# Loading and splitting the first part of two weight matrices in another place

## The chip, the cores and the metric

The kernel runs on one core of one Trainium2 chip, as a single program. The metric is the device time of one execution in microseconds (us). Before the change it is 689.38 us, the median of 3 runs (688.5 to 691.06).

## The reference

Two blocks work one after the other on an array of 2048 rows by 512 columns, both steered by a vector c (adaLN: shift, scale and gate come from `silu(c) @ w_mod`):

```
h = layernorm(u) * (1 + ca) + sa
x = u + ga * S4(h)                      # S4: per column a causal convolution of length 2048, K from A, B, C, dt; by FFT
h = layernorm(x) * (1 + cb) + sb
a  = gelu(layernorm(h) @ w1)            # 512 x 512
hs = shift(a) @ w2                      # four column groups, shifted by +1, -1, +2, -2 rows; 512 x 512
x1 = h + hs
y  = x1 + gelu(layernorm(x1) @ w3) @ w4 # 512 x 1376 and 1376 x 512
out = x + gb * y
```

All is float32. The matrix products with w1 to w4 are done in two parts: each float32 operand is split into a high part, rounded to the type that TensorE takes (fp32r), and a low part, the remainder, also fp32r; high times high, low times high and high times low are added up.

## The kernel before, in words

The order of all work is written out by hand: the program runs under manual scheduling, so each engine executes its instructions, and issues its DMAs, in the order of the source. A wait at the head of an engine's queue holds back all that is behind it on that engine.

In the first stage the kernel K of the convolution is made and u is normalized and transformed. In the second stage (`steps`, L1096 to L1153) 16 product steps run, 2 column halves by 8 blocks of frequencies: `spectrum_k` (L664) transforms K for a block from the tile VK[jh], with T2 and the flipped T3 as the other operand; `multiply` (L685) forms the complex product with the spectrum of u (tile us, two buffers); `back` (L695) transforms back over one axis and stores z to the DRAM array ZT, on POOL's queue, the last one in two parts on SP's and ACT's. `load_inv` (L717) brings the blocks of ZT (512 KB each, or halves of them) back as tiles ld, and `inv_half` (L726) does the inverse transform along the other axis, whose result VectorE adds to X2, the residual array. VK[1] and T3 lie in the pool c2, which lives until all inverse transforms are done; us, zc, z lie in the pool s2, which ends with the last product step (`s2x.close()`, L1154). SBUF is given to pools in stack order from two sides; pools with `reuse_waits="tile"` wait tile by tile for the last use of what lay there.

Behind L1154 the inverse transforms of the second half wait for the stores of the last step and the loads behind them. `inv_half(1, 3, 1)` reads blocks 0, 3, 4 and 7 of ZT, one half of each, and these four halves are the first that are loaded, two on SP's queue and two on ACT's (L1167 to L1169). `keep(n)` issues n matmuls whose result is not used. Then come the normalizations and `mix_half` (L929), the product with w1 for a group of 256 rows and half of the columns, its gelu into the tile go (pool gop, two buffers) and the store of go to the DRAM array GD on SP's queue.

From L1225 on w3 and w4 come in. Both stand in DRAM copies (WD). `weights` (L743) makes one pair of tiles for the high and the low part of a whole matrix; its `load` issues a DMA into the low tile and returns `split`, which copies the rounded value to the high tile on ACT (L755) and subtracts it in place on VectorE (L756). The loads, `load_w3(0)` to `load_w4(2)`, 23 in all, are issued on SP at L1230 to L1244, among the stores of go and the loads of `chan_load` (L870, the shifted rows from GD). The splits wait in a list, from which `split_w(n)` takes the next n: eight between L1255 and L1278, the other fifteen in the first channel group. `chan(g, r)` (L979), eight times, does the channel part for 256 rows: `chan_first` (w3, gelu), `chan_second` (w4).

The lines that the prediction's steps speak of:

```
        for k, i in ((3, 1), (0, 0)):
            load_inv(1, k, i, Y)
            load_inv(1, k + 4, i, S)
```

Of the kernel before, what the change touches and what calls it, by code (L numbers as in the profile page):

```python
# [7 lines left out]
F32 = mybir.dt.float32  # L8
# [98 lines left out]
def body(ctx, tc, A):  # L107
    nc = tc.nc
    V, S, P, T, Y = nc.vector, nc.scalar, nc.gpsimd, nc.tensor, nc.sync
# [10 lines left out]
    WD = {k: dpool.tile(list(A[k].shape), F32, name="D" + k) for k in ("w2", "w3", "w4")}  # L120
# [150 lines left out]
    f2 = lambda t: t.rearrange("p a b -> p (a b)")  # L271
# [234 lines left out]
    side = {k: [] for k in range(40)}  # L506
    for k in range(8):
        w, i = ("w3", k) if k < 4 else ("w4", k - 4)
        n = A[w].shape[0] // 4
# [37 lines left out]
    with tc.manual_schedule():  # L547
# [13 lines left out]
        for k in range(33):  # L561
# [8 lines left out]
            if k < 32:  # L570
# [3 lines left out]
                e = products(k)  # L574
# [22 lines left out]
        for f in later:  # L597
# [7 lines left out]
    c2 = a2.enter_context(pool("c2"))  # L605
# [1 line left out]
    Gm = c2.tile([128, 2, 64], F32, name="Gm")  # L607
    FI = c2.tile([128, 32, 2, 32], F32, name="FI")
    VK = [v0x.enter_context(pool("v0", side="right")).tile([128, 64, 2, 64], F32, name="VK0"),
          c2.tile([128, 64, 2, 64], F32, name="VK1")]  # L610
    ldp = a2.enter_context(pool("ldp", bufs=7))
    s2x = ExitStack()
    s2 = s2x.enter_context(pool("s2", bufs=2))
    psa = s2x.enter_context(pool("psa", bufs=2, space=PSUM))
    psb = s2x.enter_context(pool("psb", bufs=4, space=PSUM))
    kbank = lambda shape: psb.tile(shape, F32, name="pk2")
# [39 lines left out]
    t3s = {}  # L656

    def flip(kc):
        t = t3s[kc] = c2.tile([128, 8, 64], F32, name="T3", bufs=3)
        for gh in range(2):  # L660
            r = slice(gh * 64, gh * 64 + 64)
            P.tensor_scalar(t[r], T2[kc // 4][r, kc % 4 * 4:kc % 4 * 4 + 8, 64 - gh * 64:128 - gh * 64], -1.0, None, op0=OP.mult)
# [80 lines left out]
    def weights(pl, src, rows, cols, name, ntile):  # L743
        hi = pl.tile([128, ntile, cols], F32R, name=name + "h")
        lo = pl.tile([128, ntile, cols], F32R, name=name + "l")

        def load(stage, i, m=1, c0=0, c1=cols):
            n = min(128, rows - i * 128)
            w = stage(m, c1 - c0) if stage else lo.bitcast(F32)[:, i:i + m, c0:c1]
            Y.dma_start(w[:n], src[i * 128:i * 128 + (m - 1) * 128 + n, c0:c1].rearrange("(a p) n -> p a n", p=n))  # L750

            def split():
                for j in range(m):
                    h = hi[:n, i + j, c0:c1]
                    act(h, w[:n, j])  # L755
                    V.tensor_sub(lo[:n, i + j, c0:c1], w[:n, j], h.bitcast(F32))  # L756
            return split
        return hi, lo, load
# [24 lines left out]
    def half_stat(b, jh):  # L783
        V.bn_stats(st1[:, (b + 2) % 16, jh], X2[:, b, jh * 256:jh * 256 + 256])
# [50 lines left out]
    def three(p, wh, wl, hl, c):  # L835
        hi, lo = hl
        for k in range(4):
            T.matmul(p, wh[:, k, c], hi[k], start=(k == 0), stop=False)  # L838
            T.matmul(p, wl[:, k, c], hi[k], start=False, stop=False)  # L839
        for k in range(4):  # L840
            T.matmul(p, wh[:, k, c], lo[k], start=False, stop=(k == 3))  # L841
# [93 lines left out]
    def chan_first(hl, f2):  # L935
        p = psw.tile([128, 2, 256], F32, name="pm")
        ne, m = (2, 128) if f2 < 5 else (1, 96)
        for e in range(ne):
            c = slice((f2 * 2 + e) * 128, (f2 * 2 + e) * 128 + m)
            three(p[:m, e], W3h, W3l, hl, c)  # L940
        gf = c2p.tile([128, 2, 256], F32, name="gf")
        gh = c2p.tile([128, 2, 256], F32R, name="gh")
        gl = c2p.tile([128, 2, 256], F32R, name="gl")
        act(gh[:m, :ne], p[:m, :ne], AF.Gelu_apprx_tanh)
        act(gf[:m, :ne], p[:m, :ne], AF.Gelu_apprx_tanh)
        V.tensor_sub(gl[:m, :ne], gf[:m, :ne], gh[:m, :ne].bitcast(F32))  # L946
        return gh, gl, ne, m

    def second_high(acc, part, f2, i):
        gh, gl, ne, m = part  # L950
        s = slice(i * 128, i * 128 + 128)
        for e in range(ne):
            f = f2 * 2 + e
            T.matmul(acc[i], gh[:m, e, s], W4h[:m, f], start=(f == 0), stop=False)  # L954
            T.matmul(acc[i], gh[:m, e, s], W4l[:m, f], start=False, stop=False)  # L955

    def second_low(acc, part, f2, i):
        gh, gl, ne, m = part
        s = slice(i * 128, i * 128 + 128)
        for e in range(ne):  # L960
            f = f2 * 2 + e
            T.matmul(acc[i], gl[:m, e, s], W4h[:m, f], start=False, stop=(f == 10))  # L962

    def chan_second(acc, part, f2):
        for i in range(2):
# [113 lines left out]
            chan_out(g, acc, i, (Y,) if g < 7 else (Y, S))  # L1079
        return r  # L1080

    splits = []

    def load_w3(c):
        for i in range(4):
            splits.append(ldw3(None, i, 1, 512 * c, min(512 * c + 512, 1376)))

    def load_w4(c):
        for f in range(4 * c, min(4 * c + 4, 11)):
            splits.append(ldw4(None, f))  # L1090

    def split_w(n):
        for _ in range(n):
            splits.pop(0)()

    steps = [(jh, kc) for jh in range(2) for kc in range(8)]  # L1096
    with tc.manual_schedule():
# [11 lines left out]
        for n, st in enumerate(steps):  # L1109
            p = spectrum_k(*st)  # L1110
# [15 lines left out]
            if n % 2 == 0 and n < 14:  # L1126
                flip(steps[n + 2][1])
# [27 lines left out]
        tp = lambda name, bufs=1, **k: pool(name, bufs, reuse_waits="tile", **k)  # L1155
        cm = ctx.enter_context(tp("cm", 2, side="right"))
        hv = ctx.enter_context(tp("hv", side="right"))
        gop = ctx.enter_context(tp("gop", 2, side="right"))
        psT = ctx.enter_context(tp("psT", space=PSUM))
        psw = ctx.enter_context(tp("psw", 2, space=PSUM))  # L1160
        psy = a2.enter_context(tp("psy", 2, space=PSUM, side="right"))
# [12 lines left out]
            inv_half(0, 2, i, psy, "py")()  # L1174
        for b in (14, 15, 4, 5, 6, 7):
            half_stat(b, 0)
        for k in (1, 2):
            load_inv(1, k)
            load_inv(1, k + 4)
# [16 lines left out]
        hl = parts_of(transposed(mh.pop(7)[0]))  # L1196
# [10 lines left out]
        hl = parts_of(transposed(mh.pop(0)[0]))  # L1207
# [10 lines left out]
        hl = parts_of(transposed(mh.pop(1)[0]))  # L1218
# [4 lines left out]
        a2.close()  # L1223
        a12.close()
        pw34 = ctx.enter_context(tp("pw34"))  # L1225
        W3h, W3l, ldw3 = weights(pw34, WD["w3"], 512, 1376, "w3", 4)
        W4h, W4l, ldw4 = weights(pw34, WD["w4"], 1376, 512, "w4", 11)
        c2p = ctx.enter_context(tp("c2p", 2))
        psm = ctx.enter_context(tp("psm", 2, space=PSUM))
        load_w3(0)  # L1230
        mix_half(1, hl, 0)
        mix_norm(2)
        first_stats(3)
        mix_half(1, hl, 1)
        chan_load(0)
        load_w4(0)
        mix_mod1(3)
        mix_mod2(3, 0)
        hl = parts_of(transposed(mh.pop(2)[0]))
        mix_mod2(3, 1)  # L1240
        load_w3(1)
        load_w4(1)
        load_w3(2)
        load_w4(2)  # L1244
        mix_half(2, hl, 0)
        chan_split(0)
        mix_norm(3)
# [4 lines left out]
        add0()  # L1252
        hl = parts_of(transposed(mh.pop(3)[0]))
        add1 = chan_sum(0, 1)
        split_w(1)  # L1255
        n = cm.tile([128, 2, 512], F32, name="h2")
        sm = [(cm.tile([128, 2], F32, name="cmv"), cm.tile([128, 1], F32, name="crs")) for i in range(2)]

# [5 lines left out]
            V.tensor_scalar(n[:, i], cn[0][:, i], sm[i][0][:, 0:1], sm[i][1], op0=OP.subtract, op1=OP.mult)  # L1264

        stat0(0)
        split_w(1)
        add1()
        mix_half(3, hl, 0)
        stat0(1)  # L1270
        norm0(0)
        norm0(1)
        split_w(1)
        mix_half(3, hl, 1)
        r = transposed(n)
        split_w(1)
        r = parts_of(r)
        split_w(4)  # L1278
        chan_add(0)
        first_stats(4)  # L1280
        chan_load(1)
# [20 lines left out]
```

## Time and profile before

| | us |
|---|---|
| median of 3 runs | 689.38 |
| the profiled execution: its own time | 691.26 |
| the profiled execution: span | 689.5 |
| TensorE busy with matmuls | 642.6 (93%), 7195 instructions |
| VectorE (DVE) busy | 498.0 (72%), 795 |
| ScalarE (ACT) busy | 331.2 (48%), 505 |
| GpSimd (POOL) busy | 124.8 (18%), 236 |

A profile is one execution, recorded by the hardware. The span lies between the first and the last instruction recorded. PE is TensorE, PEld its weight loads, SP the queue that issues most DMAs. Busy time of a pipelined engine is not the same as use of its peak. The granted clock is the share of TensorE's full clock that it was given: 1.00 is 2.4 GHz, 0.50 is 1.2 GHz. The DMA share is the mean busy share of the core's 16 DMA engines. An arrow after a wait names what ended it as far as the profile can tell; of several things waited for it is the last by the profile, and where the one named can't have been waited for, it was another, often a DMA.

### The profile page before, as it was taken

How to read it: one execution, taken by the hardware profiler on the slowest of the kernel's cores; microseconds unless marked ns; L12 is line 12 of the kernel's file. 1: busy time of each engine (PE TensorE's matmuls, PEld its weight loads, DVE VectorE, ACT ScalarE, POOL GpSimd, SP SyncE). 2: the span in 40 equal slices, each digit the busy share in tenths (PEclk: the TensorE clock that was granted, in tenths of full speed). 3: DMA queues.
4: the chain of work that ended last, by engine and by line, in shares of the span. 5: the costliest groups of instructions: out<-in, count | busy, mean ns of one | idle time of the engine just before them, and what ended most of it. 6: DMA issues, size and time to landing. Idle time of an engine off the chain costs nothing.

```text
span 689.5 us, 16884 instructions
## 1 busy us (share of the span) xinstructions
PE 642.6 (93%) x7195; PEld 509.2 (74%) x7195; DVE 498.0 (72%) x795; ACT 331.2 (48%) x505; POOL 124.8 (18%) x236
## 2 busy tenths in 40 slices
PE   1899999999999998977998999999999999999996
PEld 0456655655569776634887889999899889898895
DVE  7899999999996887986987967464574536363522
ACT  3878988889875557432444623123131312222121
POOL 4011112112103355413741101001010000000000
PEclk9999999999999999998999999999999999999999
DMA  8603264643739997967387010020100201010001
GB/s 299 284 2 79 75 218 105 209 121 85 275 85 317 354 335 258 346 204 226 108 257 240 1 32 32 16 77 15 47 31 17 77 1 62 1 49 13 1 31 31
DMA packets 51091, 86.42 MB, mean 125 GB/s; under 512 B 4676, under 2 KB 39496, under 8 KB 48424
## 3 DMA queue, kind: packets, MB, share of 16 engines
q1 hardware_dynamic: 46712, 66.74, 30.1%
q0 software_dynamic: 3440, 17.57, 7.4%
q8 instruction: 56, 0.92, 0.6%
q10 hardware_dynamic: 864, 1.05, 0.5%
q14 instruction: 19, 0.16, 0.1%
HBM read 59.12 MB, written 32.90 MB: 133 GB/s over the span
## 4 chain that ended last, share of the span: by engine, by line
PE 70%; DVE 6%; DMA 5%; ACT 3%; POOL 2%; issue 1%; ACTq 0%; SPq 0%; DVEq 0%; POOLq 0%
PE pm L841 7%; PE pm L838 7%; PE pm L839 7%; PE xx L448 7%; PE pa L954 6%; PE pa L955 6%; PE pa L962 6%; PE kp L498 3%; DMA ZT<-z 3%; PE ph L893 2%; PE ph L895 2%; PE ph L892 2%; DMA ld<-ZT 2%; PE pu L426 2%; PE pT L803 2%; PE pk L626 2%
## 5 line engine op out<-in xcount | busy, mean ns | idle before, releaser
L115 ACT ACTIVATE gh<-pm 128x512 fp32r<-128x512 f32 (+1 forms) x48 | 26.9, 560 | 200.7 <-PE pm L841 200.7
L838 PE MATMUL pm<-nh,w3h 128*128 128x256 f32 (+1 forms) x352 | 86.6, 281 | 2.7 <-ACT nh L115 2.7
L839 PE MATMUL pm<-nh,w3l 128*128 128x256 f32 (+1 forms) x352 | 86.3, 280 | 0.1
L946 DVE TENSOR_TENSOR gl<-gf,gh 128x512 fp32r<-128x512 f32 (+1 forms) x48 | 30.8, 643 | 68.4 <-ACT gf L115 68.4
L954 PE MATMUL pa<-w4h,gh 128*128 128x512 f32 (+1 forms) x176 | 69.6, 395 | 0.0
L838 PEld LDWEIGHTS pm<-nh,w3h 128*128 128x128 f32 (+1 forms) x352 | 66.0, 187 | 4.4 <-ACT nh L115 2.9
L955 PE MATMUL pa<-w4l,gh 128*128 128x512 f32 (+1 forms) x176 | 68.9, 392 | 0.0
L839 PEld LDWEIGHTS pm<-nh,w3l 128*128 128x128 f32 (+1 forms) x352 | 65.9, 187 | 2.2 <-DVE w3l L756 0.5
L765 POOL TENSOR_TENSOR rs<-mv,eps_t 128x1 f32<-128x1 f32 (+1 forms) x39 | 11.0, 282 | 282.4 <-DVE mv L771 265.4
L841 PE MATMUL pm<-nl,w3h 128*128 128x256 f32 (+1 forms) x352 | 55.0, 278 | 0.0
L449 PE MATMUL xx<-MG,ON 64*128 64x512 f32 x160 | 48.1, 397 | 0.0
L962 PE MATMUL pa<-w4h,gl 128*128 128x512 f32 (+1 forms) x176 | 48.0, 390 | 0.0
L448 PE MATMUL xx<-MG,ON 64*128 64x512 f32 x160 | 48.0, 396 | 0.0
L841 PEld LDWEIGHTS pm<-nl,w3h 128*128 128x128 f32 (+1 forms) x352 | 47.0, 187 | 0.0
L898 DVE TENSOR_TENSOR h<-h,ph 128x512 f32<-128x512 f32 x16 | 11.0, 687 | 45.1 <-PE ph L895 45.1
L466 DVE SCALAR_TENSOR_TENSOR e<-tr,p 128x512 f32<-128x512 f32 x64 | 41.1, 684 | 1.5 <-ACT tr L115 1.5
L498 PEld LDWEIGHTS kp<-e,e 128*32 128x32 f32 x2048 | 30.1, 110 | 12.7 <-issue 7.6
L475 DVE TENSOR_TENSOR e<-tr,p 128x1024 f32<-128x1024 f32 x32 | 39.0, 1220 | 0.0
L476 DVE TENSOR_TENSOR e<-tr,m 128x1024 f32<-128x1024 f32 x32 | 39.0, 1219 | 0.0
L115 ACT ACTIVATE p<-xx 128x1024 f32<-128x1024 f32 (+1 forms) x40 | 37.5, 979 | 2.2 <-PE xx L252 1.0
L962 PEld LDWEIGHTS pa<-w4h,gl 128*128 128x128 f32 (+1 forms) x176 | 33.0, 188 | 7.3 <-DVE gl L946 0.2
L115 ACT ACTIVATE tr<-xx 128x1024 f32<-128x1024 f32 x32 | 33.0, 1030 | 9.6 <-PE xx L449 7.9
(236 smaller groups left out, 1731.6 us busy)
## 6 DMA issues: line engine op xcount, KB each, us to landing
VU<-vs SPq DMA_DIRECT2D x64, 128.0 KB, 3.7
ld<-VU SPq DMA_DIRECT2D x16, 512.0 KB, 7.4
ZT<-z POOLq DMA_DIRECT2D x30, 256.0 KB, 6.2
ld<-ZT SPq DMA_DIRECT2D x12, 512.0 KB
Dw<-in_w POOLq DMA_DIRECT2D x8, 688.0 KB, 4.7
xu<-in_u SPq DMA_DIRECT2D x4, 1024.0 KB, 8.0
KX<-in_x SPq DMA_DIRECT2D x4, 1024.0 KB, 8.0
GD<-go SPq DMA_DIRECT2D x16, 256.0 KB, 2.3
```

The source lines that it names most:

```text
L115: return S.activation(out, in_, f, bias=bias, scale=scale)
L448: T.matmul(x[:, :512], la, ma, start=(i == 0), stop=(i == len(ops) - 1))
L449: T.matmul(x[:, 512:], lb, mb, start=(i == 0), stop=(i == len(ops) - 1))
L466: V.scalar_tensor_tensor(e0[:, 1, a], tr[:, 1, 0], 1.0 - 2.0 * a, mg[:, a], op0=OP.mult, op1=OP.mult)
L475: V.tensor_mul(e0[:, 0], tr[:, 0, 0:1].to_broadcast([128, 2, 512]), mg)
L498: T.matmul(kp[32 * j:32 * j + 32, (k % 2) * 4 + g], e1[:, r, d], e0[:, r, :, d * 32:d * 32 + 32], start=(r == 0), stop=(r == 1), skip_grou ...
L838: T.matmul(p, wh[:, k, c], hi[k], start=(k == 0), stop=False)
L839: T.matmul(p, wl[:, k, c], hi[k], start=False, stop=False)
L841: T.matmul(p, wh[:, k, c], lo[k], start=False, stop=(k == 3))
L954: T.matmul(acc[i], gh[:m, e, s], W4h[:m, f], start=(f == 0), stop=False)
L955: T.matmul(acc[i], gh[:m, e, s], W4l[:m, f], start=False, stop=False)
L962: T.matmul(acc[i], gl[:m, e, s], W4h[:m, f], start=False, stop=(f == 10))
```

## The change

VK[1] and T3 move from c2 to s2, so that their place is free when the last product step ends. w3 and w4 are no longer one pair of tiles each but three, for 512, 512 and 352 columns (w3) or rows (w4). The first pair of each gets a pool of its own, pw3a, on the right side behind gop, opened right after the last product step. Its eight loads, 256 KB each, are issued there: w3's four on POOL's queue, w4's four on ACT's, ahead of the loads of the inverse transform. All eight are split by `split_w(8)` behind the half statistics that fill the time until those loads land. The other pairs are loaded on SP where they were, and the eight calls of `split_w` ahead of the channel groups are gone.

```diff
     VK = [v0x.enter_context(pool("v0", side="right")).tile([128, 64, 2, 64], F32, name="VK0"),
-          c2.tile([128, 64, 2, 64], F32, name="VK1")]
+          None]
...
+    VK[1] = s2.tile([128, 64, 2, 64], F32, name="VK1", bufs=1)
...
-        t = t3s[kc] = c2.tile([128, 8, 64], F32, name="T3", bufs=3)
+        t = t3s[kc] = s2.tile([128, 8, 64], F32, name="T3", bufs=3)
...
-        def load(stage, i, m=1, c0=0, c1=cols):
+        def load(stage, i, m=1, c0=0, c1=cols, q=Y):
...
-            Y.dma_start(w[:n], src[i * 128:i * 128 + (m - 1) * 128 + n, c0:c1].rearrange("(a p) n -> p a n", p=n))
+            q.dma_start(w[:n], src[i * 128:i * 128 + (m - 1) * 128 + n, c0:c1].rearrange("(a p) n -> p a n", p=n))
...
-            c = slice((f2 * 2 + e) * 128, (f2 * 2 + e) * 128 + m)
-            three(p[:m, e], W3h, W3l, hl, c)
+            f = f2 * 2 + e
+            three(p[:m, e], *W3[f // 4][:2], hl, slice(f % 4 * 128, f % 4 * 128 + m))
...
-    def load_w3(c):
+    splits, W3, W4 = [], [], []
+
+    def load_w3(pl, q=Y):
+        c0 = 512 * len(W3)
+        c1 = min(c0 + 512, 1376)
+        W3.append(weights(pl, WD["w3"][:, c0:c1], 512, c1 - c0, f"w3{c0}", 4))
         for i in range(4):
-            splits.append(ldw3(None, i, 1, 512 * c, min(512 * c + 512, 1376)))
-
-    def load_w4(c):
-        for f in range(4 * c, min(4 * c + 4, 11)):
-            splits.append(ldw4(None, f))
+            splits.append(W3[-1][2](None, i, q=q))
+
+    def load_w4(pl, q=Y):
+        r0 = 512 * len(W4)
+        r1 = min(r0 + 512, 1376)
+        W4.append(weights(pl, WD["w4"][r0:r1], r1 - r0, 512, f"w4{r0}", (r1 - r0 + 127) // 128))
+        for f in range((r1 - r0 + 127) // 128):
+            splits.append(W4[-1][2](None, f, q=q))
...
         gop = ctx.enter_context(tp("gop", 2, side="right"))
+        pw3a = ctx.enter_context(tp("pw3a", side="right"))
+        load_w3(pw3a, P)
+        load_w4(pw3a, S)
...
         for b in (14, 15, 4, 5, 6, 7):
             half_stat(b, 0)
+        split_w(8)
         for k in (1, 2):
             load_inv(1, k)
             load_inv(1, k + 4)
...
         pw34 = ctx.enter_context(tp("pw34"))
-        W3h, W3l, ldw3 = weights(pw34, WD["w3"], 512, 1376, "w3", 4)
-        W4h, W4l, ldw4 = weights(pw34, WD["w4"], 1376, 512, "w4", 11)
...
-        load_w3(0)
         mix_half(1, hl, 0)
...
-        load_w4(0)
...
-        load_w3(1)
-        load_w4(1)
-        load_w3(2)
-        load_w4(2)
+        load_w3(pw34)
+        load_w4(pw34)
+        load_w3(pw34)
+        load_w4(pw34)
...
         add1 = chan_sum(0, 1)
-        split_w(1)
...
         stat0(0)
-        split_w(1)
...
         norm0(1)
-        split_w(1)
         mix_half(3, hl, 1)
         r = transposed(n)
-        split_w(1)
         r = parts_of(r)
-        split_w(4)
         chan_add(0)
```

The matmuls on w4 change in the same way as those on w3 (`W4h[:m, f]` becomes `W4[f // 4][0][:m, f % 4]`).

## Rows read from the trace of the kernel before

**Rows 1.** Chain that ended last: start us, us, engine, tile, line.

```profile
308.51 4.98 DMA ld<-ZT
313.63 2.42 PE py L731 x17
...
352.67 1.18 DVE nl L811 x2
```

**Rows 2.** Windows around the hole: stretch, busy per engine, PE clock, DMA share, GB/s.

```profile
302.00:309.00 7.00, 4.85 (x46) 2.07 (x42) 5.70 (x13) 1.09 (x2) 0.00 (x0) 1.00 0.43 113
309.00:320.00 11.00, 6.37 (x64) 3.48 (x64) 3.79 (x9) 0.00 (x0) 1.91 (x4) 0.69 1.01 326
```

**Rows 3.** Timeline in the hole: start, us, engine, line, operation, [idle before].

```profile
299.61 1.07 POOL L706 DMA_DIRECT2D ZT<-z  x2 [3.10 <-ACT z L115]
...
301.36 0.69 DVE L692 TENSOR_TENSOR zc<-mb 128x512 f32<-128x512 f32 x1
...
303.93 1.18 SPq L706 DMA_DIRECT2D ZT<-z  x2
...
304.37 1.26 ACTq L706 DMA_DIRECT2D ZT<-z  x2
...
307.94 0.95 ACTq L721 DMA_DIRECT2D ld<-ZT  x2
308.35 12.13 SPq L721 DMA_DIRECT2D ld<-ZT  x10
...
316.07 0.69 DVE L734 TENSOR_TENSOR KX<-py,KX 128x512 f32<-128x512 f32 x1 [7.69 <-PE py L731]
...
317.62 0.19 POOL L765 TENSOR_TENSOR rs<-mv,eps_t 128x1 f32<-128x1 f32 x1 [16.94 <-DVE mv L789]
...
322.66 0.82 ACT L115 ACTIVATE h<-h,nm,rs 128x512 f32<-128x512 f32 x1 [18.32 <-POOL nm L828]
```

**Rows 4.** Timeline of SP, 345 to 367 us.

```profile
345.38 1.86 SPq L750 DMA_DIRECT2D w3l<-Dw  x4
...
354.24 1.86 SPq L750 DMA_DIRECT2D w4l<-Dw  x4
...
363.81 1.71 SPq L750 DMA_DIRECT2D w4l<-Dw  x3
365.93 0.88 SPq L850 DMA_DIRECT2D GD<-go  x2
```

**Rows 5.** Windows of the load burst, and of the channel part.

```profile
354.00:370.00 16.00, 16.00 (x113) 14.92 (x114) 11.66 (x20) 5.67 (x9) 3.67 (x9) 1.00 1.02 336
...
362.00:368.00 6.00, 6.00 (x41) 5.47 (x40) 5.71 (x12) 2.05 (x4) 1.55 (x4) 1.00 1.06 390
...
450.00:690.00 240.00, 233.88 (x1500) 210.86 (x1498) 115.25 (x189) 55.35 (x103) 12.38 (x32) 1.00 0.10 31
```

**Rows 6.** Timeline where the channel part begins, ACT and TensorE.

```profile
370.65 1.04 PE L803 MATMUL pT<-ident,h 128*128 128x128 f32 x8
371.71 0.60 ACT L115 ACTIVATE go<-pm 128x512 f32<-128x512 f32 x1 [7.66 <-PE pT L803]
372.20 0.62 ACT L115 ACTIVATE w3h<-w3l 128x512 fp32r<-128x512 f32 x1
...
373.72 1.08 ACT L115 ACTIVATE nh<-pT 128x512 fp32r<-128x512 f32 x2
...
374.37 0.58 PE L838 MATMUL pm<-nh,w3h 128*128 128x256 f32 x1 [2.69 <-ACT nh L115]
```

**Rows 7.** Windows behind the pause and after it.

```profile
374.40:376.40 2.00, 2.00 (x9) 2.00 (x10) 2.00 (x5) 2.00 (x5) 0.00 (x0) 0.50 0.94 230
378.00:380.00 2.00, 2.00 (x20) 2.00 (x19) 1.97 (x4) 1.25 (x3) 0.00 (x0) 1.00 0.00 0
```

**Rows 8.** Tile w3l, its splits: count, ns min/median/max, first and last start.

```profile
L115 ACT ACTIVATE w3h<-w3l x12: 495/629/633, 362.9 to 395.4; 128x512 fp32r<-128x512 f32 x8, 128x352 fp32r<-128x352 f32 x4
L756 DVE TENSOR_TENSOR w3l<-w3l,w3h x12: 520/682/693, 363.8 to 396.3; 128x512 fp32r<-128x512 f32 x8, 128x352 fp32r<-128x352 f32 x4
```

More of the change, by code (lines that the diff above doesn't have):

```diff
@@ L953, in second_high @@
             f = f2 * 2 + e
-            T.matmul(acc[i], gh[:m, e, s], W4h[:m, f], start=(f == 0), stop=False)
-            T.matmul(acc[i], gh[:m, e, s], W4l[:m, f], start=False, stop=False)
+            T.matmul(acc[i], gh[:m, e, s], W4[f // 4][0][:m, f % 4], start=(f == 0), stop=False)
+            T.matmul(acc[i], gh[:m, e, s], W4[f // 4][1][:m, f % 4], start=False, stop=False)
     def second_low(acc, part, f2, i):
@@ L961, in second_low @@
             f = f2 * 2 + e
-            T.matmul(acc[i], gl[:m, e, s], W4h[:m, f], start=False, stop=(f == 10))
+            T.matmul(acc[i], gl[:m, e, s], W4[f // 4][0][:m, f % 4], start=False, stop=(f == 10))
     def chan_second(acc, part, f2):
@@ L1080, in chan @@
         return r
-    splits = []
-    def load_w3(c):
-        for i in range(4):
-            splits.append(ldw3(None, i, 1, 512 * c, min(512 * c + 512, 1376)))
-    def load_w4(c):
-        for f in range(4 * c, min(4 * c + 4, 11)):
-            splits.append(ldw4(None, f))
+    splits, W3, W4 = [], [], []
[3 more added lines that the diff above has]
+        W3.append(weights(pl, WD["w3"][:, c0:c1], 512, c1 - c0, f"w3{c0}", 4))
+        for i in range(4):
+            splits.append(W3[-1][2](None, i, q=q))
[5 more added lines that the diff above has]
+            splits.append(W4[-1][2](None, f, q=q))
     def split_w(n):
```

## The prediction

> **What bounds the kernel now.** I read the page first: TensorE is busy 93% of the span, and from 450 us on it works 233.9 of 240 us [rows 5], so a step that only shortens another engine there gives nothing. Then the chain that ended last, in order of time, to see where it leaves TensorE. Near the change it does so twice. The first place is the hole behind the last product step: the chain goes from the load ld<-ZT, 4.98 us, to the first inverse matmuls at 313.63 us [rows 1]. Ahead of that load stand only the stores of z, so the reader is to see two DMA hops between the last product and those matmuls, with all engines waiting. The windows say what the DMA engines do: from 302 to 309 us they are busy 43% of the time, from 309 to 320 us 101% [rows 2]. The timelines say who issues what: the stores on SP and ACT at 303.9 and 304.4, the first four half loads on ACT at 307.9 and SP at 308.35; ACT sits idle 18.3 us, VectorE 7.7 us, and POOL does nothing between 300.7 and 317.6 [rows 3].
>
> The second place is at 371 us, where the channel part begins. SP issues 19 weight loads, w4 and w3 by turns, from 354.2 to 365.5 us, and the two stores GD<-go stand behind them, issued only at 365.9 [rows 4]. The DMA engines are full, 102% over 354 to 370 us [rows 5]. ACT's next evacuation into go comes at 371.71, after 7.66 us of idling [rows 6]. The profile puts that wait down to the transposes, but these come later in the program than go and can't release it; go has two buffers (L1158), so it is the store of the older go, issued at 365.9 [rows 4], that has to land. Behind that go ACT does go, a w3 split, go, a w3 split and only then nh, and TensorE waits 2.69 us for nh [rows 6]. After the pause its granted clock is 0.50, the lower of its two levels: 9 matmuls in 2 us against 20 at the full clock [rows 7].
>
> **The change part by part.** *Matmuls.* The same number, shapes and operands; only the tiles are cut differently. Zero.
>
> *VK1 and T3 in s2.* Same sizes; their last readers, the products of step 15, are done before the multiplication of that step ends at 302.05 [rows 3]. At the other end VK1 now lies over other tiles of the stage before, which TensorE and VectorE have left by then in their own order. Zero; bounds minus 0.3 and plus 0.5 us, about one DMA issue or one VectorE instruction (0.95 / 2 us [rows 3]; 0.68 [rows 8]).
>
> *Eight loads moved: 2.1 MB.* Four of w3 on POOL, behind its last store, so at 300.7; two store issues take 1.07 us [rows 3], four loads about 2.1, until 302.8. Nothing stands behind them on POOL until 317.6. Four of w4 on ACT behind its stores, 304.37 plus 1.26: 305.6; two load issues took 0.95, so four take 1.9, until 307.5, just before ACT wants to issue the ld loads at 307.94 [rows 3]. By the sizes the tiles that they fill lie over VK1, T3 and the us buffer of step 14, all read to the end by 302 [rows 3], so no wait of note is added; were one to last past 305.6, the ld issues and the splits would queue behind it. So the issues cost nothing, the bytes do. With the DMA engines to themselves such loads ran at 390 GB/s over 362 to 368 us [rows 5]: 2.1 MB are 5.4 us. The lull of 302 to 309 us has (1 - 0.43) x 7 = 4.0 us to give [rows 2]. 1.4 us are left over, 2.3 if the rate is the 326 GB/s of 309 to 320 (6.4 us) [rows 2]. What is left over is w4, on ACT's queue ahead of two of the four halves that the first inverse needs (it reads blocks 0, 3, 4 and 7, one half of each, exactly the four that are issued first). So it delays the path. I take 1.6 us, near the lower end since loads of the same shape give the 390. Ends: 0.4 us (only the landing of the z stores is pushed a little) and 6.4 us (nothing fits into the lull).
>
> *Eight splits moved.* Each is an ACT copy of 0.63 and a VectorE subtraction of 0.68 us [rows 8], eight in a row 5.0 and 5.5 us. They are queued ahead of VectorE's addition at 316.07. ACT is free from 308.9 and VectorE from 316.07 - 7.69 = 308.4 [rows 3]. The w3 part lands before 308 and is split by about 312. The last of w4 lands before the ld halves behind it, and needs 1.3 us to be split; TensorE needs 2.4 us from the halves' landing (313.63 [rows 1]) to the addition (316.07 [rows 3]). So they hide, at zero; without that cover each w4 part that lands late costs 0.7 us on the path. TensorE waits for none of them there.
>
> *What follows the hole*, up to 354 us, is a chain of VectorE, POOL, ACT and TensorE in turn (its last link before TensorE fills up is VectorE's at 352.67 [rows 1]), so 1.6 us there stay 1.6 us.
>
> *SP's queue at 345 to 366 us.* Gone are the four w3 loads at 345.4 and the first four of the 19, so 15 are left [rows 4]. I let them start at 354.2 as before, since what stands ahead of them on SP is fed by ACT. The burst shrinks from 4.6 to 3.5 MB: 1.05 MB at 336 GB/s [rows 5] are 3.1 us. The store of go lands at about 368.6 instead of 371.7. ACT can evacuate the first go once its matmuls end near 368, the second at 370.7. nh then starts when the first half of the transposes is through, at about 371.3, and TensorE at about 371.95 instead of 374.37 [rows 6]: 2.4 us. The pause shrinks to about 0.3 us, so the clock should stay at 1.00. Of the slow stretch (374.4 to 377.1, some 12 matmuls at 9 per 2 us, which take 1.2 us at 20 per 2 us [rows 7]) 1.4 us come back. Together 3.8 us. Late next is TensorE itself: it is fed without a break from there on, so this stays to the end. Bounds: 1.0 us (the stores still late, only two splits of about 0.5 us apiece fewer ahead of nh) and 4.3 us (also the last 0.3 us and small waits for w3l).
>
> Sum: 1.6 - 3.8 = -2.2 us. The profiled execution took 691.26 us (span 689.5), so 689.1 for it; the median of the runs lies 1.9 us lower, and there I predict 689.4 - 2.2 = 687.2 us.
>
> **The rivals.** *The lull swallows the loads.* For: 302 to 309 us is 57% idle [rows 2], and what SP issues behind the first halves may be held back. Against: w4 can't start before 305.6. Then 0 to 0.6 us are lost: -3.2 to -3.8, 685.9 us.
>
> *The queues take turns.* If the DMA engines serve ACT's and SP's queue alternately, the 1.6 us of w4 that stand ahead of the ACT halves go at half speed, and SP's later halves take the rest. The loss doubles to 3.2 us: -0.6, 688.8 us. For: both queues have work at once from 308.35 [rows 3], with the engines full [rows 2]. Against: SP's own first halves need half of the time anyway, so turns cost less than double. The Trainium skill (DMA: Bandwidth & Descriptors, section Queues, rings and completion order) says that each DMA engine goes round the queue rows that have work, a packet at a time, which is this case; no row here shows the order of packets.
>
> *The ld halves wait for nearly all of it (the other side).* The w3 and w4 loads start late, or run slowly beside the z stores, so that the full 2.1 MB stand before the first four halves: 5.4 to 6.4 us lost at 308 to 314 us against 3.8 gained, +1.6 to +2.6, 691.5 us. It turns slower from 3.8 us on, that is when 1.5 MB of the 2.1 are still unmoved at 309. For: the ACT loads precede the halves on their own queue. Against: the lull, and POOL's early start.
>
> *It doesn't do what it says.* ACT at 371 us waits for something else, or the stores land late all the same: gain 1.0, loss 1.6, +0.6, 690.0 us.
>
> **How the numbers follow.** Forecast 0.50 (own range 686.4 to 688.4), lull swallows 0.20, turns 0.13, whole load ahead 0.10, no gain at 371 us 0.07. A measurement of this kernel can tell about 0.5%, 3.4 us, from no change: faster is under 686.0, slower over 692.8. Half of the second case (0.10), and of the first the tail in which the gain is near its bound of 4.3 (0.12), give faster 0.22. The far end of the fourth is +2.6, so slower needs something more that I have not seen, a wait in the stage before or a later start of both loads: 0.08. The rest, 0.70, is the same. The range reaches into both neighbours: 685.0 to 691.0 us.
>
> **What would show it.** Right: POOL and ACT issue w3 and w4 at about 301 and 306 us; the DMA share of 302 to 309 us rises from 0.43 towards 0.9; the first inverse matmul comes 1 to 2.5 us after 313.6; at the start of the channel part TensorE pauses under 0.6 us at clock 1.00, and the GD<-go stores are issued right behind 15 loads. Wrong: the first inverse matmul over 3.8 us late; VectorE's addition released by a split instead of TensorE; a pause of 2 us before the first channel matmul still there; or a wait in the stage before, where VK1 moved.

## The result: 2.8 us slower, and the profile after

The changed kernel takes 691.6 us, the median of 15 runs (688.93 to 694.21), against 688.84 us for the kernel before in the same session (15 runs, 687.22 to 691.06). The ratio is 1.0033, 95% interval 1.0018 to 1.0048: slower by 2.8 us between the medians and by 2.3 us by the ratio, where 2.2 us of gain were forecast, with a range of 685.0 to 691.0 us. The profiled execution took 692.81 us, its span is 691.0.

Both places of the prediction moved, and a third one, the channel part's matmuls, that the prediction had at zero. First the hole. The chain of the changed kernel, to be held against [rows 1] (start us, us, what):

```profile
303.55 3.61 DMA ZT<-z
...
307.81 6.36 DMA ld<-ZT
...
315.17 5.38 DMA ld<-ZT
...
320.69 2.85 PE pm L732 x32
323.54 4.11 PE pT L1175 x14
...
327.78 1.06 PE pT L804 x8
```

The reader is to see three DMA hops where there were two: behind the first load stands a second ld<-ZT that SP could issue only at 315.17 (the profile puts SP's wait ahead of these loads, 4.7 us, down to the landing of an earlier ld<-ZT), and behind that the filler of 14 matmuls, which TensorE has to run before the transposes. The timeline says how it came to that (it answers to [rows 3]):

```profile
299.07 2.18 POOL L751 DMA_DIRECT2D w30l<-Dw  x4
...
302.46 1.18 SPq L707 DMA_DIRECT2D ZT<-z  x2
...
304.28 2.38 ACTq L751 DMA_DIRECT2D w40l<-Dw  x4
...
307.39 0.91 ACTq L722 DMA_DIRECT2D ld<-ZT  x2
307.81 16.02 SPq L722 DMA_DIRECT2D ld<-ZT  x10
308.34 2.19 ACT L115 ACTIVATE w30h<-w30l 128x512 fp32r<-128x512 f32 x4 [5.47 <-DMA w40l<-Dw]
...
311.42 2.49 DVE L757 TENSOR_TENSOR w40l<-w40l,w40h 128x512 fp32r<-128x512 f32 x4
...
315.31 3.38 PE L732 MATMUL py<-ld,FI 128*32 128x256 f32 x32 [9.61 <-DMA ld<-ZT]
317.44 0.69 DVE L735 TENSOR_TENSOR KX<-py,KX 128x512 f32<-128x512 f32 x1 [3.53 <-PE py L732]
```

The issues and the splits went as predicted: POOL at 299, ACT at 304, the last split done at 313.9, ahead of the addition at 317.44, which TensorE releases and no split. But the last z store left SP at 302.46 here and at 303.93 before [rows 3], so places are best counted from there: the first ld follows after 5.35 us (4.42 before), the first inverse matmul after 12.85 (9.70), nh after 25.98 (21.26). The windows against [rows 2]:

```profile
302.00:309.00 7.00, 3.37 (x38) 1.60 (x28) 4.23 (x10) 1.53 (x4) 0.00 (x0) 0.92 0.96 322
309.00:320.00 11.00, 3.38 (x32) 2.57 (x32) 7.36 (x15) 3.61 (x7) 0.93 (x3) 0.58 0.77 241
```

The lull is filled, 0.96 where it was 0.43, but behind it the DMA engines are no longer full, 0.77 against 1.01: the loads that were left weren't issued yet.

The second place did what was forecast. SP has 15 loads, from 356.97, and ACT's go is now put down to the store; the rows answer to [rows 4] and [rows 6]:

```profile
366.35 0.88 SPq L851 DMA_DIRECT2D GD<-go  x2
```

```profile
371.24 0.60 ACT L115 ACTIVATE go<-pm 128x512 f32<-128x512 f32 x1 [5.17 <-DMA GD<-go]
...
373.70 1.03 PE L804 MATMUL pT<-ident,h 128*128 128x128 f32 x8
...
374.44 1.08 ACT L115 ACTIVATE nh<-pT 128x512 fp32r<-128x512 f32 x2
...
375.09 0.39 PE L839 MATMUL pm<-nh,w30h 128*128 128x256 f32 x1 [0.35 <-ACT nh L115]
```

From the transposes to the first channel matmul it is 1.39 us, and was 3.72; TensorE waits 0.35 us instead of 2.69, and the granted clock stays at 1.00 (windows, to be held against [rows 7]):

```profile
370.00:380.00 10.00, 9.65 (x81) 9.36 (x80) 5.66 (x11) 3.80 (x8) 0.97 (x3) 1.00 0.37 116
```

The third place is the channel part, where TensorE is busy nearly all the time in both kernels. Its length can be read exactly between two instructions that come once in a group, the first matmul of the last 96 rows of w3, in the first group and in the eighth. Before:

```profile
406.92 0.28 PE L838 MATMUL pm<-nh,w3h 128*96 128x256 f32 x1
...
678.17 0.28 PE L838 MATMUL pm<-nh,w3h 128*96 128x256 f32 x1
...
618.17 0.28 PE L838 MATMUL pm<-nh,w3h 128*128 128x256 f32 x1
...
619.53 0.28 PE L838 MATMUL pm<-nh,w3h 128*128 128x256 f32 x1
```

After:

```profile
405.94 0.28 PE L839 MATMUL pm<-nh,w31024h 128*96 128x256 f32 x1
...
679.95 0.28 PE L839 MATMUL pm<-nh,w31024h 128*96 128x256 f32 x1
...
620.73 0.28 PE L839 MATMUL pm<-nh,w30h 128*128 128x256 f32 x1
...
622.17 0.28 PE L839 MATMUL pm<-nh,w30h 128*128 128x256 f32 x1
...
626.41 0.28 PE L839 MATMUL pm<-nh,w3512h 128*128 128x256 f32 x1
...
627.78 0.28 PE L839 MATMUL pm<-nh,w3512h 128*128 128x256 f32 x1
```

Seven groups took 271.25 us and take 274.01, 2.76 more: as much as the medians differ by, since the other two places nearly cancel. The other rows say where: 12 matmuls with w30 as weights take 1.44 us (0.120 each), 12 with w3512 1.37 (0.114), and before 12 with w3 1.36. With w40 moving, 512 columns, one takes 0.234 us, with w4512 0.228. Same number, shapes and operands, and slower.

### The profile page after: what moved, and what is told of

It is laid out like the page before. It is cut to its first block, busy times and chain, and to the rows that moved or that the text cites. A ratio compares the mean times of both kernels' runs of the same rounds, so it can differ in the third digit from the quotient of the medians.

```text
span 691.0 us, 16882 instructions
## 1 busy us (share of the span) xinstructions
PE 643.2 (93%) x7195; PEld 511.3 (74%) x7195; DVE 498.5 (72%) x795; ACT 330.9 (48%) x505; POOL 126.0 (18%) x240
## 4 chain that ended last, share of the span: by engine, by line
PE 78%; DVE 5%; DMA 3%; ACT 2%; POOL 2%; issue 1%; SPq 0%; ACTq 0%; POOLq 0%; DVEq 0%
PE xx L448 9%; PE pm L842 8%; PE pm L839 8%; PE pm L840 8%; PE pa L956 6%; PE pa L955 6%; PE pa L963 6%; PE kp L498 4%; PE pu L426 2%; PE ph L894 2%; PE ph L896 2%; PE ph L893 2%; PE pk L681 2%; PE pk L627 2%; PE xx L252 2%; DMA ZT<-z 2%
## 5 line engine op out<-in xcount | busy, mean ns | idle before, releaser
L681 PE MATMUL pk<-VK,xu 64*64 64x128 f32 x768 | 37.2, 271 | 0.0
L115 ACT ACTIVATE tr<-xx,hpi 128x1024 f32<-128x1024 f32 x32 | 35.8, 1118 | 2.1 <-PE xx L449 0.5
L498 PE MATMUL kp<-e,e 128*32 128x64 f32 x2048 | 35.2, 221 | 0.0
L681 PEld LDWEIGHTS pk<-VK,xu 64*64 64x64 f32 x768 | 33.0, 133 | 2.0 <-issue 1.0
L448 PEld LDWEIGHTS xx<-MG,ON 64*128 64x128 f32 x160 | 30.2, 189 | 5.4
L145 POOL TENSOR_TENSOR lur<-lum,eps_t 128x1 f32<-128x1 f32 x16 | 8.1, 509 | 140.0 <-DVE lum L143 140.0
L839 PE MATMUL pm<-nh,w1h 128*128 128x256 f32 x128 | 32.3, 286 | 0.3 <-ACT nh L115 0.3
L839 PE MATMUL pm<-nh,w30h 128*128 128x256 f32 x128 | 32.1, 284 | 0.4 <-ACT nh L115 0.4
L115 ACT ACTIVATE z<-pz 128x512 f32<-128x512 f32 x32 | 17.4, 598 | 31.0 <-PE pz L703 15.9
L840 PE MATMUL pm<-nh,w30l 128*128 128x256 f32 x128 | 32.0, 283 | 0.0
```

The costliest lines, as they stand in the source:

```text
L115: return S.activation(out, in_, f, bias=bias, scale=scale)
L448: T.matmul(x[:, :512], la, ma, start=(i == 0), stop=(i == len(ops) - 1))
L498: T.matmul(kp[32 * j:32 * j + 32, (k % 2) * 4 + g], e1[:, r, d], e0[:, r, :, d * 32:d * 32 + 32], start=(r == 0), stop=(r == 1), skip_grou ...
L681: T.matmul(p[gh][kk * 64:kk * 64 + 64, i, ro], w, VK[jh][rows, ri * 32 + k1].rearrange("p j g -> p (j g)"), start=(ri == 0), stop=(ri == 1 ...
```

## The experiments

Fifteen kernels were run. Ratios are to the kernel before, run beside them on the same chip, where it took 688.84 to 689.39 us. All stretches below are from one profile each: from SP's last z store to its first ld, to the first inverse matmul, to nh; from nh to the mark of the first group; and over the seven groups.

| kernel | MB ahead of ZT loads | ld | inverse | nh | nh to mark | 7 groups | us | ratio (95%) |
|---|---|---|---|---|---|---|---|---|
| before | 0 | 4.42 | 9.70 | 21.26 | 81.73 | 271.25 | 688.84 | |
| changed | 2.1 | 5.35 | 12.85 | 25.98 | 77.50 | 274.01 | 691.6 | 1.0033 (1.0018-1.0048) |
| e1 | 0 | 4.44 | 8.80 | 20.58 | 81.86 | 271.26 | 689.84 | 1.0006 (0.999-1.0021) |
| e2 | 0 | 4.45 | 9.51 | 21.07 | 81.26 | 274.01 | 692.23 | 1.0037 (1.0018-1.0056) |
| e3 | 2.1 | 8.57 | 12.79 | 24.55 | 77.70 | 274.02 | 692.63 | 1.0044 (1.0029-1.0058) |
| e4 | 1.05 + part | 7.03 | 11.74 | 27.64 | 79.19 | 274.02 | 692.42 | 1.0054 (1.0033-1.0076) |
| e6 | 0 | 4.45 | 9.37 | 20.75 | 79.82 | 274.02 | 690.56 | 1.0016 (0.9999-1.0033) |
| e7 | 1.05 | 5.16 | 10.26 | 22.03 | 80.50 | 274.02 | 691.26 | 1.0038 (1.002-1.0056) |
| e8 | 2.1 | 4.95 | 12.40 | 23.71 | 78.60 | 274.02 | 691.75 | 1.0038 (1.0022-1.0054) |
| e11 | 2.1 | 5.25 | 12.29 | 23.75 | 77.61 | 271.77 | 689.42 | 1.001 (0.9992-1.0027) |
| e12 | 0 | 4.45 | 8.56 | 20.34 | 79.98 | 272.07 | 687.83 | 0.9981 (0.9967-0.9994) |
| e13 | 0 | 4.45 | 9.95 | 21.19 | 79.44 | 269.87 | 685.0 | 0.9944 (0.9923-0.9964) |
| e14 | 0 | 4.44 | 9.02 | 20.80 | 81.64 | 269.93 | 687.85 | 0.9977 (0.9963-0.999) |
| e15 | 0 | 4.46 | 8.90 | 20.57 | 83.42 | 274.61 | 692.47 | 1.0048 (1.0031-1.0065) |

**e1, the move of VK1 and T3 alone.**

```diff
-          c2.tile([128, 64, 2, 64], F32, name="VK1")]
+          None]
+    VK[1] = s2.tile([128, 64, 2, 64], F32, name="VK1", bufs=1)
-    t = t3s[kc] = c2.tile([128, 8, 64], F32, name="T3", bufs=3)
+    t = t3s[kc] = s2.tile([128, 8, 64], F32, name="T3", bufs=3)
```

> Only VK1 and T3 lie in the pool s2, as in the changed kernel; w3 and w4 stay as before. In the one pair of profiles the changed kernel sends its last z out 1.47 us earlier than the kernel before (302.46 against 303.93 us). Theory (the move of VK1 and T3 does this): about 687.4 us, and the last z store of SP near 302.5 us. Rival (it is the scatter from execution to execution, and the move is worth nothing, as predicted): 688.8 us, within 0.5.

689.84 us, no difference, and the z store at 303.67 us. The 1.47 us by which the changed kernel was ahead there is scatter between executions: over the kernels of this study that store lies between 301.3 and 303.9 us, and e15, which leaves VK1 and T3 where they were, has it at 301.7.

**e2, the places without the early load.**

```diff
-        load_w3(pw3a, P)
-        load_w4(pw3a, S)
+        load_w3(pw3a, None)     # makes the tiles only
+        load_w4(pw3a, None)
...
-        split_w(8)              # and the split_w calls of the kernel before
...
+        get_w3(0)               # ahead of mix_half(1, hl, 0): four loads on SP
...
+        get_w4(0)               # behind chan_load(0)
```

> The tiles and places of the changed kernel (first pair of w3 and w4 in pw3a, VK1 and T3 in s2), but loaded on SP and split where the kernel before does it. So neither the hole's loss nor the gain at 371 us is there. Theory (matmuls are slower when the first pair's weights lie at pw3a's place): the groups with w30 and w40 keep a spacing of 0.120 and 0.234 us where w3512 and w4512 have 0.1135 and 0.228, the channel part is 2.0 us longer than before, and the time is 690.8 us (689.3 if the move of VK1 and T3 is worth 1.5). Rival (the spacing comes from what runs beside these groups, or from the early load): spacing as before, 688.8 us.

By the table the hole and the start of the channel part are close to before, the seven groups take 274.01 us, as in the changed kernel to the hundredth, and the ratio of 1.0037 is 2.6 us. So the new tiles at their new place, with no load ahead of the halves, make the kernel slower by as much as the whole change does; e11 and e15 below part the place from the cut into three.

**e3, w4 through POOL, and e4, the calls behind the ZT loads.**

```diff
# e3
-        load_w4(pw3a, S)
+        load_w4(pw3a, P)
# e4
-        load_w3(pw3a, P)
-        load_w4(pw3a, S)
...
         for k, i in ((3, 0), (0, 1)):
             load_inv(1, k, i)
             load_inv(1, k + 4, i)
+        load_w3(pw3a, P)
+        load_w4(pw3a, S)
```

> The changed kernel with w4's four early loads on POOL, behind w3's four, and not on ACT. Theory (the second four halves of ZT came late because SP's loads shared a ring of eight semaphores with w4's four loads of ACT, and so each waited for one of them): SP issues its ten loads within 13 us (12.13 before, 16.02 in the changed kernel), none of them waits for w40, the second KX additions come 2 to 3 us earlier, and the time is 689.0 to 689.8 us. Rival (only the 2 MB stand in the way, through whichever queue they go): 691.6 us, or more, since POOL needs 2.2 us for each of its issues and the splits come later.

> The changed kernel with the calls that load w3 and w4 put behind the loads of the eight ZT halves: POOL's four of w3 go out as early as before, but ACT's four of w4 now stand behind its two ZT halves, and SP's halves no longer take their semaphores behind w4's. Theory (the order on the semaphore ring and on ACT's queue made the loss): the first inverse matmul comes 1 to 2 us earlier, the second four halves 3 us earlier, and the time is 688.6 to 689.6 us. Rival (bytes alone): the transfers overlap all the same, 691.0 to 691.6 us.

My theory of the hole fell with both. In e3 nothing on ACT or SP stands behind w4 any more, and SP issues its ten loads in 10.51 us, faster than before the change. It helps nothing (timeline of e3):

```profile
299.06 2.18 POOL L751 DMA_DIRECT2D w30l<-Dw  x4
...
301.23 1.59 POOL L751 DMA_DIRECT2D w40l<-Dw  x3
302.45 1.18 SPq L707 DMA_DIRECT2D ZT<-z  x2
...
310.59 0.95 ACTq L722 DMA_DIRECT2D ld<-ZT  x2
311.02 10.51 SPq L722 DMA_DIRECT2D ld<-ZT  x10
...
315.24 4.29 PE L732 MATMUL py<-ld,FI 128*32 128x256 f32 x32 [9.55 <-DMA ld<-ZT]
```

Now it is the stores that come late: the ld loads wait for them to land, 8.57 us instead of 4.42. Whatever queue carries the 2.1 MB, the first inverse matmul stands 12.8 us behind the store. (The rival's 2.2 us of POOL are for four issues, not for one, as the first row shows.) In e4 half goes out early through POOL and the rest between the halves; nh is later still, at 27.64, but that profiled execution took 695.81 us, 3.4 above the median of e4, and may not be typical.

**e7, half the bytes, and e6, none ahead.**

```diff
# e7: load_w4's first part back to its old place; split_w(4) in the hole
# e6: both loads behind the last four ZT loads, on SP; splits where before has them
         for k in (1, 2):
             load_inv(1, k)
             load_inv(1, k + 4)
+        get_w3(0)
+        get_w4(0)
         keep(6)
```

> The changed kernel with only w3's part in the hole (1 MB, through POOL, its four splits there); w4's part is loaded and split where the kernel before does it, into the changed kernel's place. Theory (the bytes stand in front of the z stores and the ZT loads): half of the hole's loss, the first inverse matmul 11 to 11.5 us behind SP's z store (9.7 before, 12.85 changed), and about half of the gain at 371 us: 691 us. Rival (the loss came from w4's loads on ACT's queue and on its semaphores): no loss in the hole, 689.5 us.

> The places of the changed kernel, but the first pair is loaded by SP right behind the last four ZT loads, and split where the kernel before does it. Theory (the 2 MB cost the hole 3 to 4 us only because they come before the ZT loads; between 320 and 340 us the DMA share is 0.2 to 0.4, so there they are free; the gain at 371 us of 3.3 us stays; the place costs 2.3 us): 1 us below the kernel before, 688.4 us. Rival (the gain at 371 us came from the early splits, not from the early load): 2.3 us above before, 691.7 us.

In the order of the change and of e7 the loss grows with the bytes: nh comes 20.3 to 21.3 us behind the store in the eight kernels with none in front, 22.03 with 1.05 MB, 23.7 to 26.0 with 2.1 MB in the order of the change (three profiles) and 24.55 through POOL; e4 with its 27.64 is outside of that order. e7's first inverse matmul, at 10.26, came earlier than the 11 to 11.5 us expected. e7 gains about as much at the second place as it loses. In e6 the hole is free and part of the gain is there: nh to mark 79.82, 1.9 us less than before. Its loads at 318.82 and 321.40 lie where the DMA engines had time (windows of e6; before had 0.20 in the third):

```profile
302.00:309.00 7.00, 3.42 (x38) 1.67 (x30) 4.30 (x10) 0.94 (x2) 0.00 (x0) 1.00 0.58 157
309.00:320.00 11.00, 8.11 (x71) 5.45 (x72) 5.65 (x12) 0.00 (x0) 2.79 (x6) 0.69 0.93 304
320.00:330.00 10.00, 9.56 (x87) 7.59 (x86) 9.69 (x22) 5.18 (x7) 5.15 (x17) 1.00 0.77 258
```

I expected 688.4 us and got 690.56: the gain of the second place was put in with 3.3 us, of which 1.9 are there, and the place cost 2.8 us, not 2.3. The five kernels with all eight splits in the hole (changed, e3, e4, e8, e11) have nh to mark between 77.5 and 79.2, those with the loads behind the ZT loads and late splits (e6, e12, e13) between 79.4 and 80.0. So the rest probably needs the splits out of the way too; no run moves the splits alone.

**e8, the filler cut from 14 to 4.**

```diff
-        keep(14)
+        keep(4)
```

> The changed kernel with the second filler of 14 matmuls cut to 4 (their results go nowhere). In the changed kernel's profile the filler runs from 323.5 to 327.65 us, after halves that came late, and the transposes start at 327.78 us although the first normalised h was there before. Theory (the filler, being in order behind the late halves, is on the path): 1.5 to 1.9 us below the changed kernel, about 690 us. Rival (the transposes wait for h anyway, or the clock falls without the filler): 691.6 us or more.

691.75 us, no gain. The nh of this profile, 23.71, looks 2.3 us better, but e11, which has the changed kernel's hole instruction by instruction with all 14, has 23.75: one profile of the hole scatters by 2 us. The filler stood on the path in the profile shown above; in e11 the chain goes through VectorE and POOL instead. That cutting it is worth anything isn't shown.

**e5, e9 and e10: what makes the matmuls slow.** Three probes of one execution each, read by their traces and not by their times.

```diff
...
+        hx = hl[0][0]           # nh; gm, not shown, is a tile at gh's place
+        for wt in (W1h, W2h, W3[0][0], W4[0][0], W3[1][0], W4[1][0], W4[2][0]):
+            for mv in (hx, gm[:, 0], W2h[:, 3, 256:512], ...):
+                p = psw.tile([128, 2, 256], F32, name="pm")
+                for i in range(12):
+                    T.matmul(p[:, 0], wt[:, i % 2, i // 2 % 4 * 128:i // 2 % 4 * 128 + 128], mv, start=True, stop=True)
```

> The changed kernel with 42 groups of 12 matmuls appended behind its last product (extra work whose results nothing uses): each of seven weights (w1, w2, and the five high parts w30, w40, w3512, w4512, w41024) against each of six moving operands (nh, gh, and columns of w2, w1, w40, w3512), all 128x128 by 128x256 and with no other engine at work. Theory (the place of the weights alone sets the spacing): the groups with w1, w2, w30 and w40 as weights stand at 0.120 us, those with w3512, w4512 and w41024 at 0.1135 us, whatever moves. Rival 1 (it is the pair of places): the spacing of one weight changes with the moving operand. Rival 2 (what the other engines do beside it): 0.1135 us in all of them.

The spacing is a matter of the pair, and of no other engine (timeline of e5, moving operand first):

```profile
701.28 1.60 PE L1295 MATMUL pm<-nh,w30h 128*128 128x256 f32 x12
702.72 1.58 PE L1295 MATMUL pm<-gh,w30h 128*128 128x256 f32 x12
...
718.38 1.53 PE L1295 MATMUL pm<-nh,w3512h 128*128 128x256 f32 x12
719.75 1.58 PE L1295 MATMUL pm<-gh,w3512h 128*128 128x256 f32 x12
```

From start to start w30 needs 1.44 us against nh, w3512 1.37 against nh and 1.42 against gh. w2 is fast against gh (1.38) and w3512 (1.37), slow against nh (1.43).

```diff
+        for w in tl:            # 13 tiles of 16 KB (the last 15)
+            for m in tl:
...
+                for i in range(12):
+                    T.matmul(p[:, :256], w[:, i % 4 * 128:i % 4 * 128 + 128], m[:, 512:768], start=True, stop=True)
```

> None of the work is done: thirteen tiles of 16 KB (15 KB the last) fill the memory of a partition from byte 16512 up, and each serves once as weights (four blocks of its first 2 KB in turn) against each of the thirteen as moving operand (from its byte 2048): 12 matmuls of 256 columns for each pair, then 6 of 512. In the appended groups the left-side weights were fast (0.114 us) with nh alone, w1 and w2 with w3512 alone, w30 and w40 with nothing (0.118 to 0.120). Theory (the two places together decide: the operands must lie in different stretches of the memory): a map of blocks, 0.1135 us where the two tiles lie in different stretches and 0.119 where they share one. Rival (it is not the place, but what was written there or when): one spacing for all pairs.

The theory of blocks fell: 0.120 us at 256 columns for all pairs, 0.227 at 512 for all but one. Among these places, which stretch of the memory an operand lies in doesn't matter. But these places were all alike in their low address bits, and the fast pairs of e5, by the addresses in the built program, were not: nh starts at byte 96 modulo 256, w30h at 96 too, w3512h at 160.

```diff
+                for i in range(12):
+                    c = a * 16 + i % 4 * 128      # weights from byte 64 a
+                    T.matmul(p[:, :256], w[:, c:c + 128], m[:, b * 16:b * 16 + 256], start=True, stop=True)
```

> None of the work is done. In the map of whole stretches all 169 pairs of places had one spacing (0.120 us at 256 columns, 0.227 at 512), and there all places were alike modulo 512 bytes. Here sixteen weights whose first block starts at byte offsets 0, 64, ... 960 (modulo 1024) stand against sixteen moving operands at the same sixteen offsets, 12 matmuls of 256 columns for each pair and 6 of 512. In the appended groups of the changed kernel the fast pairs are just those where the weights start 64 bytes (modulo 512) behind the moving operand. Theory (the difference of the two addresses modulo some 512 bytes decides): stripes along the diagonal, 0.1135 us where the weights start 64 bytes behind and 0.118 to 0.120 elsewhere; at 512 columns 0.227 at difference 0 and 0.232 to 0.234 at 128 and 320. Rival (data, history or order decide): 0.120 and 0.227 everywhere.

One weight (from byte 64) against the moving operands from byte 0, 64, 128, ... (timeline of e10):

```profile
55.04 1.57 PE L128 MATMUL pm<-ma,wb 128*128 128x256 f32 x12
56.45 1.60 PE L128 MATMUL pm<-mb,wb 128*128 128x256 f32 x12
57.89 1.58 PE L128 MATMUL pm<-mc,wb 128*128 128x256 f32 x12
59.30 1.58 PE L128 MATMUL pm<-md,wb 128*128 128x256 f32 x12
60.72 1.52 PE L128 MATMUL pm<-me,wb 128*128 128x256 f32 x12
62.08 1.58 PE L128 MATMUL pm<-mf,wb 128*128 128x256 f32 x12
```

1.41, 1.44, 1.41, 1.42, and 1.36 against me. Stripes with a period of 256 bytes: the 64 pairs whose weights start 64 bytes behind the moving operand modulo 256 have 115.3 ns in the mean (113.3 to 117.5), the other three offsets 118.5, 118.5 and 118.1. At 512 columns it is offset 0 that is best, 230.1 against 231.5 to 233.3 ns. The offset is not all: ma and me above both have the good one, and take 1.41 and 1.36. And e9, with offset 0 in all pairs, has 120.0 and 226.7 ns where e10 has 118.5 and 230.1 at that offset.

**e11 and e12, 192 unused bytes.** They bring w30 and w40 from byte 96 to byte 160 modulo 256.

```diff
+        pw3a.tile([128, 48], F32, name="pad")
```

> The changed kernel with 192 unused bytes behind the first pair in pw3a, so that w30h, w30l, w40h and w40l start at byte 416 modulo 512 like the left-side weights, and not at 96. Theory (the place counts modulo 512 bytes only): w30 and w40 return to 0.1135 and 0.228 us, the seven groups take 271.3 us and not 274.0, and the time is that of the changed kernel less 2.8 to 3.1, about 688.7 us: within 0.3% of the kernel before. Rival (the stretch of memory or the side decides): 691.6 us, groups 274.0.

> The kernel that loads the first pair behind the last four ZT loads (690.6 us, 1.0016 of the kernel before), with the same 192 bytes. Theory (the two effects are independent): 2.8 to 3.1 us less, about 687.6 us, 0.997 to 0.998 of the kernel before. Rival (place by side or stretch): 690.6 us.

With 192 bytes the changed kernel's groups take 271.77 us, not the 271.3 expected, and its time is that of the kernel before, 1.001 (0.9992 to 1.0027). e6 with the same bytes, e12, is faster than before, 0.9981 (0.9967 to 0.9994). The pad did more than the theory says. 12 matmuls with w30 fell from 1.44 to 1.36 us, but those with w3512, which the pad doesn't move (its address and nh's are the same in both built programs), rose from 1.37 to 1.41 (timeline of e11):

```profile
622.58 0.28 PE L839 MATMUL pm<-nh,w3512h 128*128 128x256 f32 x1
...
623.99 0.28 PE L839 MATMUL pm<-nh,w3512h 128*128 128x256 f32 x1
```

So one pair's spacing can change though neither operand moved. What does it, perhaps the matmuls that run before, was not tested.

**e13 to e15, unused bytes elsewhere.**

```diff
# e13 (on e6) and e14 (on before); e15 has the last line only
+        ctx.enter_context(tp("pada", side="right")).tile([128, 48], F32, name="pada")
         cm = ctx.enter_context(tp("cm", 2, side="right"))
+        ctx.enter_context(tp("padb", side="right")).tile([128, 48], F32, name="padb")
...
+        ctx.enter_context(tp("padc")).tile([128, 16], F32, name="padc")
         pw34 = ctx.enter_context(tp("pw34"))
```

> The kernel that loads the first pair behind the last four ZT loads, with 192 unused bytes above cm, 192 below it and 64 below pw34, so that w1, w3 and the first pair all start 64 bytes behind nh modulo 256, and w2 and w4 start where wh and gh do. Theory (the offset modulo 256 decides): w1's 384 matmuls of the mixing part fall from 0.1195 to 0.114 us and the 192 of w2 from 0.232 to 0.228 us, 2.1 and 0.8 us, less where VectorE sets the pace: 1.5 to 2.9 us below the kernel with the 192 bytes alone (687.8 us), about 685.7 us, 0.995 of the kernel before. Rival (the offset does not carry over to other weights): 687.8 us, 0.998.

> The kernel before, with the same unused bytes and nothing else. Theory (offset modulo 256): 1.5 to 2.9 us below the kernel before, about 687.2 us; groups of four in the channel part shorter by 48 matmuls of w1 and 24 of w2, 0.36 us, that is 43.33 to 42.97. Rival (the offset does not carry over): 689.4 us, groups 43.33.

> The kernel before, with 64 unused bytes below w3 and w4 and nothing else: w3 starts 128 bytes behind nh modulo 256 and not 64; w4 and gh move together. Theory (the offset decides): all 1056 matmuls of w3 in the channel part go from 0.1135 to 0.119 us, 5.8 us: about 695.2 us, the seven groups 276.4 and not 271.3 us. Rival (64 bytes cost nothing; the place of pw3a had something else): 689.4 us and 271.3.

64 unused bytes in the kernel before cost 3.3 us (1.0048), with the groups at 274.61. The offsets for w1 and w2 bring the kernel before to 0.9977 (0.9963 to 0.999), and with the load behind the ZT loads the time falls to 685.0 us, 0.9944 (0.9923 to 0.9964): e13 beats both kernels. So unused bytes alone, with no load moved, make this kernel faster or slower, and the effect carries over to other weights. But e15 was priced too high, at 5.8 us: its 12 matmuls take 1.41 or 1.42 us, not 1.43. And in the kernel before, the rows of w3 are 5504 bytes apart, which puts every second block at offset 192, where e10 has 118.1 ns; these were as fast as the others. With e11 this shows that the stripes are not the whole rule.

## Why the prediction was wrong

*Matmuls: "The same number, shapes and operands; only the tiles are cut differently. Zero."* This is the step that failed, and the one that made the kernel slower than before. The seven groups cost 2.76 us more, in all seven kernels that keep pw3a's offset (274.01 or 274.02), with or without the early load; 192 bytes take 1.95 (e12) to 2.24 us (e11) of it away; what stays goes with w3512, which got slower under the pad. That the tiles' place in SBUF sets the cost is shown by these pads and by e15; the rule behind it stays open. No bound stood beside that zero, though the trace of before had two values for one shape: 12 matmuls of w3 take 1.36 us (618.17 to 619.53 above) and 12 of w1 1.42 (timeline of before):

```profile
355.67 0.28 PE L838 MATMUL pm<-nh,w1h 128*128 128x256 f32 x1
...
357.09 0.28 PE L838 MATMUL pm<-nh,w1h 128*128 128x256 f32 x1
```

*Hole, +1.6 us (0.4 to 6.4).* The mechanism of bytes ahead of the path was right, the size was not. With 2.1 MB in the change's order nh comes 24.9 us behind the z store in the mean of two profiles (25.98 in the changed kernel, 23.75 in e11) against 20.8 in the mean of eight kernels without: about 4.1 us, with 2 us of scatter. (The prediction's 2.3 us at 326 GB/s is 2.4 by its own rows; it carried nothing.) I counted the lull of 302 to 309 us as 4.0 us to give. It isn't free: z's last stores run in it, and the ld loads wait for their landing. e3 shows that cost by itself, 8.57 us in place of 4.42. The Trainium skill (DMA: Bandwidth & Descriptors, section Queues, rings and completion order) says that a DMA's semaphore increment lands only after every earlier write of the same DMA engine, across its queues. The times of e3 agree with that, but plain sharing of the engines would give such a delay too, and no run here tells the two apart.

*"What follows the hole ... 1.6 us there stay 1.6 us."* In the changed kernel's profile it grew, against before, from 3.15 us at the first inverse matmul to 4.72 at nh, with the late second halves and the in-order filler on the chain. In e11, with the same instructions there, it did not: 2.59 and 2.49. So one profile went against this step and one with it. The sign of being right, that the first inverse matmul comes 1 to 2.5 us after 313.6, came true by luck: it started at 315.31, but the z store was 1.47 us early in that execution.

*Second place, -3.8 us (1.0 to 4.3).* Right: nh to mark fell from 81.73 to 77.50, 4.2 us, to 77.6 or 77.7 in e11 and e3, and to 78.60 in e8 (3.1 us).

*VK1 and T3, zero* (e1: 1.0006) *and the splits, zero* were right.

With measured terms: 4.1 - 4.2 + 2.8 = +2.7 us, measured +2.8. That the two agree so closely is partly luck, as the hole's term alone scatters by 2 us. With the matmuls nearly at zero, as in e11, hole and second place cancel, and the forecast of a gain would still have failed, by the hole. Of the rivals the one that named the whole load ahead of the halves came nearest, 691.5 us, but for another reason.

## What to carry to other kernels

A tile that moves in SBUF can change the spacing of the matmuls that read it, at the same shape and clock; where TensorE sets the pace, measure the start-to-start time of a dozen matmuls before and after, and try a pad of 64, 128 or 192 bytes; look at all tiles then, since e11's pad made one faster and another slower. A lull of the DMA engines is no room for other transfers if a store that the path waits for runs in it: put them behind the last load of the path (e6), not ahead.

## What was not expected of the hardware

The spacing of float32r matmuls depends on where their operands start: over the pairs of e10, with no other engine at work, by up to 6% at 256 columns (0.1133 to 0.1199 us) and 2% at 512 (0.2298 to 0.2348), and in the mean it follows the start of the weights against the start of the moving operand, modulo 256 bytes. The Trainium skill (SBUF — State Buffer, section Who interferes with whom) has TensorE with two independent read ports, one for the moving operand and one for the weight load. The runs here measure a dependence between the two, so the measurement decides; what in the hardware makes it stays open, and so does the full rule: in e5 w3512 against w40 stands at the good offset and takes 0.1175 us, and in e11 w3512 takes 1.41 us for 12 where w30 takes 1.36, both 64 bytes behind nh.
